# A new written-out order for one core, in which the fifth load waits for the first

## The chip, the cores and the metric

The kernel runs on one core of one Trainium2 chip. The metric is the time that the device takes for one launch, in microseconds. Three runs of the kernel before took 370.65, 370.40 and 370.61 us, the median is 370.61 us. The profile is of one further execution.

## What is computed

Three stages follow one another, on two sequences (batch 2) of 768 tokens.

1. Attention with 8 heads of 64 channels. Each query sees its neighbours at a distance under 16, and 24 summaries, one for each block of 32 tokens: the largest key and the mean value of the block. Softmax runs over both together.
2. A mixer on x (768 tokens x 512 channels): theta = x @ w_theta; y = w_tok_r @ (x cos theta) + w_tok_i @ (x sin theta); u = x + y; the stage gives u + relu(u @ w_ch).
3. A gated unit: h = gelu(x @ w_in), split into u and v of 512 channels; v is normalised over its channels, mixed over tokens by w_sg, scaled, biased, multiplied by u; the stage gives x + gated @ w_out.

## The kernel before

**A list of steps.** The program is cut into some 1,670 named steps, each on one engine. The function `op` registers a step. `play` walks a string, `PLAN`, and issues the steps in that order. A word of it reads `name.engine.place`: `k1.S.479` issues the load of the keys of pair 1 on SP (S) into place 479 of a byte-addressed area in SBUF; P is TensorE, V VectorE, A ScalarE, G GpSimd. For P, K, B and D kinds the place is a PSUM bank or a small buffer. So the order on each engine, which engine does a step that may run on several, and every buffer's place all come from `PLAN`. Nothing is scheduled at run time. A word with `~name` adds a wait on that earlier step; before the change this is used for GpSimd steps alone, to keep them behind a VectorE step.

**Pairs.** Heads go in pairs, eight pairs p = 0 to 7 (four of each sequence). A pair has one load of keys `kP` (128 x 768 f32), one of values turned `vTP` (the same size), two halves of queries `qP_0`, `qP_1` (128 x 384), and two of values by window `vP_0`, `vP_1` (96 x 774, as two transfers). All loads are issued by SP, in the order of `PLAN`.

**Steps of a pair's half.** `ksP` (VectorE) takes the block maxima of the keys. `SP_h` (TensorE, lines 636, 643, 650) makes the scores: 4 matmuls that write the masks, 24 with keys, 24 with block maxima. `mP_h` and `dP_h` (VectorE) find and subtract the maximum, `eP_h` (ScalarE) is the exponential, `PTP_h` (TensorE, line 674) transposes, `PtP_h` (ScalarE) copies out, `OP_h_0/1` (line 690) multiply by values, `nP_h` divides, `XP_h` (line 711) transposes. `vsP` (GpSimd for the first pairs, lines 583 and 585) sums values by block in five instructions, `vpP` (line 600) transposes the sums, `vmP` and `vrP_h` spread them into the value tiles, which the `O` steps read.

**Fillers.** `fill` is 97 matmuls without use before the first scores, `idleN` are matmuls of 480 columns without use (line 472), as many as the tuple `IDLE` says.

**The rest.** `th`, `y` (mixer), `ch`, `iv`, `iu`, `sg`, `o` are products in three fp32r matmuls each (lines 385 to 387). The weights of theta, `wthN`, come by load `wthNd` and three conversions. The number after each letter is the sequence. In the gated unit, `iv1_*` make v of the second sequence, `st1_*`, `sq1` and `rv1` its statistics, `vo1_i` the normalised tile i, `vn1_ih` and `vn1_il` its high and low part. `sg1_*_i` multiplies with tile i, `iu1_*` makes u, and `o0_*` is the last product of the first sequence.

Of the kernel before, what the change touches and what calls it, by code (L numbers as in the profile page):

```python
# [55 lines left out]
wth0t.A.2 vs2.G.2 e0_1.A vp2.P.3 vr0_0.G v0_1.S.1054 wth0r.V.1152 PT2_0.P.1 Pt2_0.A.1355 d1_1.V.3  # L56
k3.S.720 O0_0_0.P.6 q3_1.S.360 O0_0_1.P e2_1.A vT3.S.1536 n0_0.V.1.1632 vm2.A.1 idle2.P.0 PT0_1.P.0
O1_0_0.P.2 Pt0_1.A.96 O1_0_1.P X0_0.P.4 n1_0.V.0 xe0_0.V wth1d.S.832 v2_0.S.479 PT2_1.P.6 ks3.V.0
vr0_1.G~wth0r e1_1.A wth0h.A.1920 vs3.G.5~wth0r wth1t.A.0 v1_1.S.406 PT1_1.P.0 q3_0.S.2736 X1_0.P.4
O0_1_0.P.5 wth1r.V.687 Pt2_1.A.144 S3_1.P.2 S3_0.P.6 O0_1_1.P v3_0.S.1743 vr1_1.A Pt1_1.A.48  # L60
O1_1_0.P.0 O1_1_1.P wth0l.V m3_1.V.1 xh0_0.G.2208~wth0l vr2_0.G~wth0l d3_1.V.315 O2_0_0.P.2
O2_0_1.P wth1h.A.2696 xe1_0.A m3_0.V.4 d3_0.V.723 e3_1.A v2_1.S.783 vr2_1.G~wth0l wth2d.S.896
xh1_0.G.2064~wth0l vp3.P.1 n0_1.V.1.192 vm3.A.1 PT3_1.P.3 xl0_0.G~wth0l v3_1.S.1103 O2_1_0.P.1
O2_1_1.P n1_1.V.0 th0_0.P.6 e3_0.A Pt3_1.A.528 wth3d.S.2624 X0_1.P.7 n2_0.V.4 PT3_0.P.4
vr3_0.G~wth0l th2_0.P.0 vr3_1.G~wth0l wr1d.S.990 n2_1.V.0 X2_0.P.3 vT5.S.2448 wth2t.A.2 wr0d.S.1792
wth3t.A.1 Pt3_0.A.1055 O3_1_0.P.2 O3_1_1.P xl1_0.G xe2_0.A O3_0_0.P.5 O3_0_1.P k4.S.288 q4_1.S.1448
wi0d.S.1186 xe0_1.A X1_1.P.3 xh2_0.A.144 wth2r.V.736 wth1l.V wth2h.A.64 th2_1.P wth3r.V.2496
n3_0.V.1 X2_1.P.7 th0_1.P X3_0.P.4 q4_0.S.455 th1_0.P.5 vT4.S.2640 wri0d.S.1472 xl2_0.G~wth3r
th1_1.P wth2l.V wr0t.A.1 wri1d.S.2576 wth3h.A.0 wr1t.A.2 wth3l.V xe3_0.A th0_2.P th1_2.P
xh3_0.A.2064 xe2_1.A wr0r.V.1154 n3_1.V.2 th2_2.P X3_1.P.7 wi0t.A.1 ks4.V.1 xh0_1.G.2016~wr0r  # L70
xe1_1.A xl3_0.G~wr0r wr1r.V.544 xh2_1.A.864 th1_3.P th0_3.P wi0r.V.576 S4_0.P.1 v4_0.S.719 S4_1.P.3
th2_3.P xl0_1.V xl2_1.G~xl0_1 xe3_1.A xh1_1.G.144~xl0_1 th5_0.P.7 kk1.A.1888 rr1.V.1600 v4_1.S.1250
m4_0.V.5 xl1_1.G~xl0_1 d4_0.V.1299 th3_0.P.2 th4_0.P.5 wri0t.A.1 th3_1.P wr2d.S.2176
xh3_1.G.912~xl0_1 kk0.A.687 q7_0.S.1223 vs4.V.4 vp4.P.1 wri0r.V.1888 ab1_0.A.2144 wri1t.A.2
k6.S.1400 m4_1.V.1 d4_1.V.1747 xl3_1.G~wri0r wi0h.A.960 kk2.A.639 rr2.V.2496 th3_2.P ks6.V.1
q6_1.S.312 th3_3.P e4_0.A sc1_0.A PT4_0.P.3 vm4.A.1 wi0l.G~wri0r th4_1.P rr0.V.1792 th5_1.P
ab0_0.V.1824 th5_2.P q7_1.S.391 kk3.A.496 wri0h.G.1088~wri0r q6_0.S.2664 wri0l.G~wri0r wri1r.V.415
Pt4_0.A.2256 vs5.V.4 vr4_0.A S6_0.P.0 O4_0_0.P.6 v5_0.S.2399 rr3.V.1568 O4_0_1.P sc0_0.A vp5.P.4
e4_1.A th4_2.P zm1_0.G~wri1r v7_1.S.1487 vr4_1.G~wri1r PT4_1.P.2 th5_3.P wr0h.A.1984 ab2_0.A.447
vT6.S.671 k5.S.2544 zm0_0.G~wri1r zh0_0.G.832~wri1r Pt4_1.A.336 m6_0.V.0 wr0l.G~wri1r n4_0.V.4.2592  # L80
th4_3.P wi1d.S.2319 zl0_0.G~wri1r ks5.V.2 d6_0.V.626 q5_0.S.288 wri1h.G.768 X4_0.P.3 kk4.A.736
vm5.A.2 zh1_0.A.896 zl1_0.G rr4.V.2464 wi1t.A.2 wri2d.S.1728 O4_1_0.P.2 O4_1_1.P xe4_0.A S5_0.P.0
S6_1.P.4 vs6.V.4 y0_0_0_0.P.6.3 y0_0_0_1.P m5_0.V.0 wri1l.G d5_0.V.578 vp6.P.1 y0_0_1_0.P.0
n4_1.V.1.672 m6_1.V.0 d6_1.V.1843 k7.S.2256 y0_0_1_1.P kk5.A.512 q5_1.S.1351 S5_1.P.4 wr1h.A.1024
wr1l.G sc2_0.A y0_1_0_0.P e6_0.A wi1r.V.1186 e5_0.A ks7.V.0 vm6.V.1 PT5_0.P.1 vr5_0.A vT7.S.2128
wi1h.G.128~wi1r wi1l.G~wi1r wri2t.A.2 y0_1_0_1.P v6_0.S.1247 m5_1.V.4 Pt5_0.A.336 wr2t.A.0
d5_1.V.1403 rr5.V.288 vs7.V.4 S7_1.P.4 v5_1.S.1351 e5_1.A y0_1_1_0.P vr5_1.A e6_1.A PT5_1.P.1
wi2d.S.2311 zm2_0.G~wi1r zh2_0.G.832~wi1r y0_1_1_1.P zl2_0.G~wi1r m7_1.V.1 v7_0.S.1167 d7_1.V.1299
PT6_0.P.4 Pt5_1.A.464 O5_1_0.P.7 O5_1_1.P O5_0_0.P.1 Pt6_0.A.416 O5_0_1.P wri2r.V.1888 S7_0.P.4
wr2r.V.512 vr6_0.A wri2h.G.896~wr2r v6_1.S.591 n5_1.V.1 O6_0_0.P.2 n5_0.V.1 O6_0_1.P wri2l.G~wr2r  # L90
wr2h.A.2048 wr4d.S.2383 X5_1.P.1 e7_1.A m7_0.V.2 wr2l.G~wr2r vp7.P.7 wi2t.A.1 d7_0.V.419 xe5_1.A
vr6_1.G~wr2r vm7.A.2 y0_2_0_0.P e7_0.A n6_0.V.6 PT7_1.P.4 X5_0.P.7 wi5d.S.320 xe5_0.V wr5d.S.2240
Pt7_1.A.1296 PT7_0.P.1 vr7_1.G~wr2r Pt7_0.A.2128 vr7_0.G~wr2r PT6_1.P.4 wi2r.V.1218 X6_0.P.7
O7_0_0.P.2 wi2h.G.384~wi2r O7_1_0.P.1 O7_1_1.P Pt6_1.A.1439 ab2_1.V.2351 wi2l.G~wi2r ab1_1.A.2208
O7_0_1.P xe6_0.V wr4t.A.2 xh4_0.V.528 n7_1.V.1 O6_1_0.P.4 O6_1_1.P y0_2_0_1.P xh5_0.A.480 sc1_1.A
X7_1.P.7 n7_0.V.0 wr3d.S.1856 xl4_0.G~wi2r ab3_0.V.2544 n6_1.V.4 xl5_0.G~wi2r th8_0.P.5
ab3_1.V.1536 th8_1.P wr4r.V.1154 ab0_1.A.2112 X4_1.P.1 wr3t.A.1 xh6_0.V.1440 xe4_1.V ab4_0.A.608
th7_0.P.2 sc0_1.A xe7_1.V xl6_0.V wr3r.V.2144 sc2_1.A wi5t.A.0 wri3d.S.1280 y0_2_1_0.P X7_0.P.1
y0_2_1_1.P zm0_1.V th6_0.P.4 xe7_0.V X6_1.P.7 sc3_0.A xh4_1.G.1488~zm0_1 zm2_1.G~zm0_1 th7_1.P
xh7_0.A.528 xl7_0.V th7_2.P th6_1.P zh0_1.A.832 xe6_1.A zl0_1.V xh6_1.V.480 ab5_1.V.2176 wri3t.A.2  # L100
sc3_1.A xl4_1.G~zl0_1 xl6_1.V th8_2.P wri3r.V.640 th8_3.P xh5_1.A.1872 wr3h.A.1728 th7_3.P
kk7.A.1568 th6_2.P xl5_1.V wr3l.G~xl5_1 th6_3.P xh7_1.A.528 th11_0.P.1 zm1_1.V th11_1.P th9_0.P.7
th9_1.P th9_2.P wri4d.S.2112 wri5d.S.2383 kk6.A.1632 kk8.A.1600 zm3_0.V sc5_1.A th11_2.P rr7.V.1248
xl7_1.V th10_0.P.2 th10_1.P zm3_1.V wi5r.V.1312 rr6.V.1216 zh3_1.G.1920~wi5r ab6_0.V.320 rr8.V.1280
ab4_1.A.1568 th9_3.P th10_2.P wr4h.A.1472 wr4l.V zl3_1.V wri3h.A.448 th11_3.P zh3_0.G.64~zl3_1
wi3d.S.1600 wri4t.A.0 kk9.A.352 rr9.V.1664 zh1_1.G.2696~zl3_1 zl1_1.V zm5_1.V sc4_0.A ab8_1.A.1536
wr5t.A.1 wr5r.V.576 sc4_1.A wi5h.A.1344 ab6_1.V.1696 zl3_0.V th10_3.P wri4r.V.1152 zh2_1.A.1856
wi3t.A.1 wi3r.V.2112 wi3h.A.512 ab9_0.A.1184 zl2_1.G~wi3r wri3l.V wi3l.V wch0d.S.2240 sc6_0.A
wri5t.A.1 wi4d.S.2319 zm4_0.V y0_0_2_0.P.5.4 y0_0_2_1.P y0_0_3_0.P.7 y0_0_3_1.P y0_1_2_0.P
y0_1_2_1.P y0_1_3_0.P wri4h.A.1792 y0_1_3_1.P y0_2_2_0.P wch1d.S.2528 y0_2_2_1.P wri4l.V y0_2_3_0.P  # L110
y0_2_3_1.P wi5l.V zm4_1.G~wi5l wr5h.A.1408 zh4_0.A.2696 zh4_1.G.0~wi5l wri5r.V.1312 zm6_0.V
wi4t.A.2 y0_3_0_0.P wch2d.S.2112 wch2t.A.1 wr5l.V wi4r.V.2464 zl4_1.V ab5_0.A.1600 y0_3_0_1.P
ab8_0.V.2351 kk10.A.1152 y0_3_2_0.P y0_3_2_1.P y0_3_3_0.P zl4_0.G~zl4_1 zh5_1.G.832~zl4_1
wi4h.A.1856 rr10.V.2432 sc8_1.A kk11.A.639 y0_3_1_0.P ab9_1.A.2319 y0_3_3_1.P sc8_0.A wi4l.G~zl4_1
rr11.V.352 zh6_0.G.1920~zl4_1 y0_3_1_1.P zl5_1.V wri5h.A.64 wri5l.V wch0t.A.0 sc9_1.A sc6_1.A
sc5_0.A y0_4_2_0.P wch2r.V.2400 y0_4_2_1.P wch3d.S.576 zm8_0.G~wch2r y0_4_3_0.P ab7_0.V.1152
zm5_0.V wch1t.A.2 ab11_1.V.1280 wch0r.V.640 wch3t.A.1 zm8_1.V y0_4_0_0.P y0_4_3_1.P sc9_0.A
y0_5_2_0.P ab7_1.A.1632 zh5_0.A.2176 zm6_1.V y0_5_2_1.P y0_5_3_0.P wch1r.V.1312 y0_4_0_1.P
y0_4_1_0.P y0_4_1_1.P zh6_1.A.2240 y0_5_3_1.P zl5_0.V sc7_0.A zm7_0.G~zl5_0 zh7_0.A.0 ab11_0.A.1568
zm9_1.V ab10_1.A.2464 sc10_1.A zl7_0.V sc7_1.A y0_5_0_0.P y0_5_0_1.P winv2d.S.1216 zl6_0.V  # L120
# [1074 lines left out]
```

## Time and profile before

| | |
|---|---|
| median of the runs | 370.61 us |
| the profiled execution | 369.8 us |
| its span, first to last instruction | 368.1 us |
| TensorE matmul busy | 358.0 us (97%) |
| VectorE busy | 300.1 us (82%) |
| ScalarE busy | 215.2 us (58%) |
| GpSimd busy | 156.7 us (43%) |
| share of the chain that ended last | PE 89%, DMA 4%, DVE 2%, ACT 2% |

Some 1.7 us of the execution lie outside the span. A busy TensorE is one with a matmul in flight: matmuls overlap, so a step's cost is best read as the start of the next step less its own start. The chain is followed back from the last instruction; where it names an engine other than TensorE, TensorE was not what set the pace there.

### The profile page before, as it was taken

The page shows a single profiled execution, that of the slowest core. Times are in us where ns is not written, and L with a number is a line of the kernel's source. Part 1 is how long each engine was busy: PE and PEld are TensorE (multiplying, and loading weights), DVE is VectorE, ACT ScalarE, POOL GpSimd, SP SyncE. Part 2 cuts the span into 40 slices and gives each one's busy share as a digit, 9 for nine tenths or more (in the row PEclk, how much of TensorE's full clock was granted, in tenths as well). Part 3 has the DMA queues.
Part 4 walks back from the last instruction along what each step waited for, and adds up shares of the span by engine and source line. Part 5 has one row for each costly group of instructions (what it writes and reads, how often), then busy time and mean ns, then how long its engine had stood idle before and what let it go on. Part 6 is the DMA issues. An engine that isn't in the chain of part 4 may idle for free.

```text
span 368.1 us, 8188 instructions
## 1 busy us (share of the span) xinstructions
PE 358.0 (97%) x3237; PEld 330.9 (90%) x3237; DVE 300.1 (82%) x525; ACT 215.2 (58%) x414; POOL 156.7 (43%) x172
## 2 busy tenths in 40 slices
...
GB/s 249 334 300 379 343 231 284 153 207 116 59 164 179 57 2 239 46 116 1 2 0 2 43 59 45 42 88 58 144 0 2 0 3 57 58 2 0 61 69 215
DMA packets 16486, 40.53 MB, mean 110 GB/s; under 512 B 2240, under 2 KB 7872, under 8 KB 16448
## 3 DMA queue, kind: packets, MB, share of 16 engines
...
## 4 chain that ended last, share of the span: by engine, by line
PE 89%; DMA 4%; DVE 2%; ACT 2%; SPq 1%; POOL 1%; issue 0%; DVEq 0%
PE banks L385 27%; PE banks L386 26%; PE banks L387 26%; PE banks L690 3%; PE banks L674 2%; DMA page1F<-in_vT_dram 2%; PE banks L643 2%; DMA page14F<-in_qT_dram 2%; PE banks L711 1%; ACT banks L1026 1%; PE banks L650 1%; POOL page1F L583 1%; PE banks L636 1%; DVE page10F L1045 1%; SPq L568 1%
## 5 line engine op out<-in xcount | busy, mean ns | idle before, releaser
L372 ACT ACTIVATE page3F<-banks 128x384 f32<-128x384 f32 (+1 forms) x14 | 6.5, 468 | 19.6 <-PE banks L387 12.0
L656 DVE TENSOR_REDUCE small<-banks 128x6 f32<-128x720 f32 x16 | 14.4, 901 | 2.7 <-PE banks L650 2.6
L372 ACT ACTIVATE page1F<-banks 128x384 f32<-128x384 f32 (+1 forms) x13 | 7.7, 590 | 11.0 <-PE banks L387 9.6
L804 DVE TENSOR_TENSOR xT<-banks,xT 128x256 f32<-128x256 f32 (+1 forms) x16 | 8.1, 547 | 2.8 <-PE banks L387 2.8
L372 ACT ACTIVATE page7F<-banks 128x256 f32<-128x256 f32 (+2 forms) x15 | 7.0, 470 | 5.3 <-PE banks L387 5.2
L385 PE MATMUL banks<-page6R,page12R 128*128 128x384 f32 x24 | 8.0, 334 | 0.0
L386 PE MATMUL banks<-page6R,page12R 128*128 128x384 f32 x24 | 8.0, 334 | 0.0
L387 PE MATMUL banks<-page6R,page12R 128*128 128x384 f32 x24 | 8.0, 334 | 0.0
L380 POOL TENSOR_TENSOR page4R<-xT,page4R 128x384 fp32r<-128x384 f32 x3 | 3.1, 1021 | 11.4 <-DVE page6R L380 7.6
L1083 DVE SCALAR_TENSOR_TENSOR page1F<-banks,g_sb,page13F 128x384 f32<-128x384 f32 x10 | 6.0, 612 | 1.7 <-PE banks L387 1.6
L385 PE MATMUL banks<-page9R,page5R 128*128 128x384 f32 (+2 forms) x22 | 7.3, 333 | 0.0
L386 PE MATMUL banks<-page9R,page5R 128*128 128x384 f32 (+2 forms) x22 | 7.3, 331 | 0.0
L387 PE MATMUL banks<-page9R,page5R 128*128 128x384 f32 (+2 forms) x22 | 7.3, 330 | 0.0
L583 POOL TENSOR_TENSOR page8F<-page8F 128x384 f32<-128x384 f32 (+3 forms) x8 | 4.5, 564 | 6.0 <-DMA page8F<-in_vT_dram 5.6
L517 ACT ACTIVATE stage<-page11F 128x512 f16<-128x512 bf16 x6 | 4.7, 785 | 4.1 <-DMA page11F<-in_w_ch_dram 3.6
L380 POOL TENSOR_TENSOR page4R<-page1F,page4R 128x512 fp32r<-128x512 f32 (+1 forms) x3 | 4.4, 1480 | 5.7 <-ACT page4R L372 3.2
L875 POOL TENSOR_TENSOR page8F<-page1F,page8F 128x256 f32<-128x256 f32 x2 | 2.4, 1203 | 10.2 <-DVE page3F L875 6.2
L385 PE MATMUL banks<-page6R,page2R 128*128 128x384 f32 x20 | 6.7, 335 | 0.0
L386 PE MATMUL banks<-page6R,page2R 128*128 128x384 f32 x20 | 6.7, 335 | 0.0
L387 PE MATMUL banks<-page6R,page2R 128*128 128x384 f32 x20 | 6.7, 334 | 0.0
L875 POOL TENSOR_TENSOR page8F<-page12F,page3F 128x256 f32<-128x256 f32 x1 | 5.3, 5275 | 2.7 <-DVE page4R L380 2.7
L374 POOL TENSOR_SCALAR page7R<-xT 128x384 fp32r<-128x384 f32 (+1 forms) x2 | 1.4, 676 | 11.7 <-DVE page1F L1089 6.9
...
## 6 DMA issues: line engine op xcount, KB each, us to landing
page12F<-in_w_iT_dram SPq DMA_DIRECT2D x3, 511.8 KB, 4.3
page1F<-in_w_in_dram SPq DMA_DIRECT2D x3, 511.8 KB, 3.6
...
page1F<-in_w_sgT_dram SPq DMA_DIRECT2D x3, 384.0 KB, 3.2
page4F<-in_w_theta_dram SPq DMA_DIRECT2D x2, 511.8 KB, 6.1
page9F<-in_w_rT_dram SPq DMA_DIRECT2D x2, 511.8 KB, 5.9
page11F<-in_w_rT_dram SPq DMA_DIRECT2D x2, 511.8 KB, 5.9
page11F<-in_w_ch_dram SPq DMA_DIRECT2D x2, 511.8 KB, 4.8
```

Of the source, the lines that this page charges most:

```text
L372: ACT.activation(dst, src, AF.Copy)
L380: EN[e].tensor_tensor(out=lo, in0=src, in1=hi.bitcast(F32), op=ALU.subtract)
L385: PE.matmul(ps, ah, bh, start=first, stop=False, skip_group_check=True)
L386: PE.matmul(ps, ah, bl, start=False, stop=False, skip_group_check=True)
L387: PE.matmul(ps, al, bh, start=False, stop=last, skip_group_check=True)
L583: POOL.tensor_tensor(out=vv[:, :, :m], in0=vv[:, :, :m], in1=vv[:, :, m:2 * m], op=ALU.add)
L643: PE.matmul(s3(h)[sl(ab, 64), t, :WK], q[rr, sl(2 * t + ab, 64)], k[rr, FIRST[w]:FIRST[w] + WK], start=False, stop=True, skip_group_check= ...
L656: op(f"m{u}", "V", lambda e: DVE.tensor_reduce(out=m3(), in_=s4(), axis=AX.X, op=ALU.max, negate=True), after=[f"S{u}"], new=[(f"m{u}", "K ...
L674: PE.transpose(T(f"PT{u}")[:WC, h, sl(t)], T(f"P{u}")[:, 360 * h + t * WC:360 * h + (t + 1) * WC], ident)
L690: PE.matmul(ps[64 * ab:64 * ab + 64, o:o + 65], sb[:WC, x:x + 64], v[:WC, c:c + 65], start=True, stop=True)
L804: DVE.tensor_tensor(out=dst, in0=ps, in1=dst, op=ALU.add)
L875: op(f"{nm}+{j}", "VG", lambda e, j=j, p=p, q=q, o=o: EN[e].tensor_tensor(out=s(j)(), in0=p(), in1=q(), op=o), after=after + pre[j], cols= ...
```

## The change

The functions stay as they are. `IDLE` and the whole of `PLAN` change: the order of the steps on every engine, most places, and the engine of 185 steps out of some 1,670 (between VectorE, ScalarE and GpSimd). One filler step, `idle2`, goes; the first grows by two matmuls. The first sixteen loads before and after:

```
before: k1 q1_0 k2 vT1 q2_0 k0 q0_0 vT0 q2_1 q0_1 vT2 q1_1 v1_0 v0_0 wth0d v0_1 ...
after:  k1 q1_0 k0 k2 vT1~k1 q2_0 q0_0 vT0 q0_1 wth0d vT2 q2_1 v0_0 v1_0 q1_1 vT3 ...
```

`vT1.S.336~k1` is the fifth load. `play` gives it a wait on the landing of `k1`; SP works in order, so every later load is issued behind it. The beginning of the diff:

```diff
-IDLE = (6, 1, 1,)
+IDLE = (8, 1,)
...
-ones.V band.G k1.S.479 masks.G q1_0.S.240 warm.V.2716 identb.V fill.P.6 ks1.V.5 maskb.A S1_0.P.4
-m1_0.V.2 k2.S.1368 ks2.V.3 sets.G d1_0.V.195 vT1.S.1584 q2_0.S.599 k0.S.1296 ks0.V.4 idle0.P.0
-S2_0.P.6 m2_0.V.2 q0_0.S.1512 idle1.P.0 S0_0.P.0 d2_0.V.3 vT0.S.312 sums.G e1_0.A q2_1.S.288
-q0_1.S.72 vs1.G.1 vs0.G.0 vp1.P.4 vm1.A.0 vT2.S.1440 PT1_0.P.2 m0_0.V.1 S0_1.P.4 d0_0.V.2691
-Pt1_0.A.240 vp0.P.2 S2_1.P.6 q1_1.S.608 e2_0.A e0_0.A v1_0.S.2447 vr1_0.A PT0_0.P.0 m0_1.V.4
-d0_1.V.99 m2_1.V.1 d2_1.V.1798 S1_1.P.4 vm0.A.2 Pt0_0.A.192 v0_0.S.527 m1_1.V.4 wth0d.S.2112
...
+k1.S.2640 ones.V q1_0.S.1448 k0.S.1296 band.G warm.V.2716 k2.S.48 masks.G sums.G vT1.S.336~k1
+identb.V fill.P.6 q2_0.S.240 ks1.V.5 q0_0.S.599 ks0.V.4 maskb.A S1_0.P.4 ks2.V.3 vT0.S.144 sets.G
+idle0.P.0 S2_0.P.6 m1_0.V.2 d1_0.V.99 e1_0.A m2_0.V.0 d2_0.V.3 vs1.G.1 S0_0.P.0 vp1.P.2 m0_0.V.7
+vm1.A.0 q0_1.S.455 d0_0.V.2691 vs0.G.6 idle1.P.3 S0_1.P.2 e2_0.A PT2_0.P.6 m0_1.V.4 wth0d.S.656
+wth0t.A.2 e0_0.A vp0.P.5 vT2.S.1440 q2_1.S.1512 v0_0.S.591 vm0.A.2 S2_1.P.0 vr0_0.A PT0_0.P.4
+Pt0_0.A.2544 d0_1.V.195 v1_0.S.527 PT1_0.P.2 vs2.G.2 q1_1.S.360 S1_1.P.4 m2_1.V.8 Pt1_0.A.1536
...
```

TensorE's order at the start and around the statistics of the second sequence (the other engines' steps left out):

```
before: fill S1_0 idle0 S2_0 idle1 S0_0 vp1 PT1_0 S0_1 vp0 S2_1 PT0_0 S1_1 vp2 PT2_0 O0_0_0 ...
after:  fill S1_0 idle0 S2_0 S0_0 vp1 idle1 S0_1 PT2_0 vp0 S2_1 PT0_0 PT1_0 S1_1 O0_0_0 vp2 PT0_1 O0_0_1 O1_0_0 O1_0_1 PT2_1 X0_0 PT1_1 S3_1 O0_1_0 S3_0 ...

before: iv1_1C_1_1 iv1_1B_0_1 (14 steps of iu1) o0_0B_0_0 sg1_1_2_0 sg1_1_1_0 sg1_1_0_0 sg1_0_2_0 sg1_0_0_0 sg1_1_2_1 o0_1A_0_0 ...
after:  iv1_0C_1_0 iv1_0C_1_1 (14 steps of iu1, with o0_1A_0_0 and o0_0A_0_0 between them) o0_0B_0_0 sg1_1_2_0 sg1_0_2_0 sg1_0_0_0 sg1_1_2_1 sg1_0_0_1 ...
```

In that place `vn1_0h` and `vn1_0l` move from VectorE to GpSimd.

## Rows read from the trace of the kernel before

**Rows 1.** Busy us by stretch: PE, PEld, DVE, ACT, POOL, clock, DMA, GB/s
```profile
27.80:300.00 272.20, 272.20 (x2257) 249.91 (x2254) 223.02 (x398) 170.03 (x334) 118.39 (x112) 1.00 0.31 103
300.00:314.00 14.00, 13.08 (x75) 12.11 (x74) 12.29 (x24) 11.49 (x24) 7.97 (x7) 1.00 0.17 54
364.00:368.10 4.10, 0.00 (x0) 0.00 (x0) 0.51 (x1) 0.00 (x0) 0.00 (x0) 0.85 0.53 193
```

**Rows 2.** The chain that ended last, 0 to 30 us: start, us, what
```profile
4.05 7.67 DMA page1F<-in_vT_dram
21.21 5.54 DMA page14F<-in_qT_dram
```

**Rows 3.** TensorE's timeline, 1.5 to 28 us: start, us, line, operation, wait
```profile
1.55 3.42 PE L466 MATMUL banks<-page14F 128*128 128x40 bf16 x97 [1.55 <-DVE page14F L400]
4.89 0.35 PE L636 MATMUL banks<-maskb,identb 64*64 64x288 bf16 x4
5.99 1.39 PE L472 MATMUL banks<-maskb,identb 128*128 128x480 bf16 x6
7.31 0.32 PE L636 MATMUL banks<-maskb,identb 64*64 64x288 bf16 x4
8.73 0.72 PE L643 MATMUL banks<-page7F,page3F 64*64 64x96 f32 x24 [1.10 <-DMA page3F<-in_qT_dram]
9.70 0.38 PE L472 MATMUL banks<-maskb,identb 128*128 128x480 bf16 x1
10.01 0.32 PE L636 MATMUL banks<-maskb,identb 64*64 64x288 bf16 x4
11.93 0.28 PE L600 MATMUL banks<-ident,small 128*24 128x128 f32 x1
12.79 0.32 PE L636 MATMUL banks<-maskb,identb 64*64 64x288 bf16 x4
14.66 0.28 PE L600 MATMUL banks<-ident,small 128*24 128x128 f32 x1 [0.72 <-POOL small L585]
17.99 0.82 PE L674 MATMUL banks<-ident,page0F 128*120 128x128 f32 x6
25.46 0.32 PE L636 MATMUL banks<-maskb,identb 64*64 64x288 bf16 x4
27.76 0.57 PE L690 MATMUL banks<-page5F,page0F 120*64 120x65 f32 x12
```

**Rows 4.** Busy time by stretch, two early slices, columns as in rows 1
```profile
5.00:6.00 1.00, 1.00 (x53) 0.97 (x53) 0.00 (x0) 0.00 (x0) 0.00 (x0) 1.00 0.86 203
8.00:9.00 1.00, 0.27 (x12) 0.30 (x16) 0.89 (x2) 0.08 (x1) 0.82 (x1) 1.00 1.00 386
```

**Rows 5.** Loads: form, count, size of one, us from issue to landing
```profile
page2F<-in_kT_dram SPq DMA_DIRECT2D x1, 384.0 KB, 3.2
page11F<-in_w_theta_dram SPq DMA_DIRECT2D x1, 511.8 KB, 5.7
```

**Rows 6.** TensorE's timeline, 307 to 314 us, columns as in rows 3
```profile
307.88 0.33 PE L385 MATMUL banks<-page4R,page5R 128*128 128x384 f32 x1
308.93 0.45 PE L385 MATMUL banks<-page9R,page8R 128*128 128x384 f32 x1 [0.36 <-DVE page8R L377]
309.94 0.34 PE L385 MATMUL banks<-page9R,page8R 128*128 128x384 f32 x1
310.47 0.33 PE L385 MATMUL banks<-page9R,page8R 128*128 128x384 f32 x1
312.03 0.33 PE L385 MATMUL banks<-page0R,page2R 128*128 128x384 f32 x1
313.17 0.44 PE L385 MATMUL banks<-page11R,page0R 128*128 128x384 f32 x1 [0.46 <-DVE page3F L1065]
```

**Rows 7.** The same stretch on VectorE and on GpSimd: the low part of a tile
```profile
308.91 0.69 DVE L380 TENSOR_TENSOR page8R<-page3F,page8R 128x512 fp32r<-128x512 f32 x1
310.56 1.34 POOL L380 TENSOR_TENSOR page2R<-page3F,page2R 128x512 fp32r<-128x512 f32 x1
```

More of the change, by code (lines that the diff above doesn't have):

```diff
@@ L55 @@
-d0_1.V.99 m2_1.V.1 d2_1.V.1798 S1_1.P.4 vm0.A.2 Pt0_0.A.192 v0_0.S.527 m1_1.V.4 wth0d.S.2112
[L56 to L120, printed above, removed]
@@ L223 @@
-g0_0q2l.G o0_0B_0_0.P.5 wout1d.S.1375 vo1_1.A vn1_0h.V.1664 vn1_0l.V sg1_1_2_0.P.3 iu1_012.V.2600
-ut1_1_0g.A.264 sg1_1_1_0.P.4 vo1_4.A vo1_2.V vo1_3.V vn1_1h.G.384~vn1_0l vn1_2h.A.2432
-sg1_1_0_0.P.0 sg1_0_2_0.P.6 iu1_111.V.2688 iu1_011.V.664 vn1_3h.V.512 vn1_1l.G~vn1_0l sg1_0_0_0.P.1
-g0_1+2.G.2064~vn1_0l vn1_2l.V ut1_0_0g.A g0_1q1h.A.2112 vn1_3l.G~vn1_2l sg1_1_2_1.P o0_1A_0_0.P.2
-vn1_4h.V.2304 wout3d.S.704 vo1_5.A sg1_1_0_1.P sg1_0_0_1.P sg1_0_2_1.P sg1_1_2_2.P sg1_1_2_3.P
-o0_0A_0_0.P.7 wout1t.A.1 sg1_0_2_2.P sg1_1_0_2.P vn1_4l.V sg1_0_0_2.P sg1_0_0_3.P sg1_0_0_4.P
```

330 lines of the change are left out of this document (200 added, 130 removed).

## The prediction

> **What bounds the kernel now.** I read the chain that ended last first, then TensorE's busy time by stretch, then its timeline where the two disagree. From 27.8 to 300 us TensorE is busy all 272.2 us [rows 1]: in that time the order of the other engines costs nothing, and the new order has nothing to win there, only to lose. Time that isn't products lies in three places. At the start the chain runs through two loads, `vT0` (issued at 4.05, landed 7.67 later, at 11.72) and `q3_0` (21.21 + 5.54 = 26.75) [rows 2]. Around 308 us the statistics of the second sequence hold TensorE up [rows 1, 6]. The end, after the last product at 363.9, is one VectorE step and a store [rows 1], and both orders close with a product, a VectorE step and a store, so I put 0 on the end.
>
> What TensorE loses at the start comes from its timeline [rows 3]. A scores step takes 5.99 - 4.89 = 1.10 where its data are there. The first filler takes 7.31 - 5.99 = 1.32. `S2_0` takes 9.70 - 7.31 = 2.39, so it loses 1.29 (to `q2_0`). The single filler takes 0.31, and there is a second one alike. `S0_0` takes 11.93 - 10.01 = 1.92, loses 0.82. `S0_1` to `vp0` is 14.66 - 12.79 = 1.87, loses 0.77 (the block sums of `vT0`). `S3_0` takes 27.76 - 25.46 = 2.30, loses 1.20 (`q3_0`). Together 1.32 + 1.29 + 0.62 + 0.82 + 0.77 + 1.20 = 6.0 us. This is all that the new start can win.
>
> **The change, part by part.** *Landings after the change.* The first eight loads are the same set, so if the transfers keep their pace the eighth, `vT0`, lands at 11.72 in both [rows 2]. Inside the set `k0` moves ahead. A load of keys has 128 x 3072 B = 0.393 MB [rows 5], a half of queries 0.197, a half of window values 96 x 3096 B = 0.297, a theta weight 0.524 [rows 5]. Behind `q2_0` there then come `q0_0` and `vT0`, 0.59 MB; at the 386 GB/s of 8 to 9 us [rows 4] that is 1.5 us, so `q2_0` lands at 10.2 (before: in time for the 8.73 start [rows 3]). `vT1` lands 0.79 MB before 11.72, at 9.7. For what follows I take the pace of before: from `vT0` to `q3_0` the loads were five halves of queries, three of keys or values, five halves of window values and two theta weights, 4.70 MB in 26.75 - 11.72 = 15.0 us, 0.3125 MB/us. After the change: `q2_1` comes after `q0_1`, `wth0d`, `vT2`: 1.31 MB, 15.9. `q1_1` 0.79 MB more, 18.4. `k3` 1.51 more, 23.3. `q3_0` 0.79 more, 25.8. `v3_0` 2.24 more, 33.0.
>
> *TensorE after the change.* To 5.99 as before: `k1` and `q1_0` stay first and second. The filler of 8 costs 8/6 x 1.32 = 1.76, to 7.75. `S2_0` waits for `q2_0`: its key matmuls start 0.1 after 10.2, and from there to the next step it is 0.97 (8.73 to 9.70 [rows 3]), so 11.3: it takes 3.5, loses 2.4. `S0_0` to 12.4 without a wait (`q0_0` at 10.7). `vp1` needs the sums of `vT1`: 9.7 + 2.9 (before: 11.72 to 14.66 [rows 2, 3]) = 12.6, loses 0.2. The single filler 0.3. `S0_1` to 14.1, `PT2_0` 0.8 [rows 3], to 15.0; `vp0` waits for GpSimd, which takes `vT0` only after `vT1`: 12.6 + 2.8, loses 0.45. `S2_1` waits for `q2_1` at 15.9, loses 0.25. `S1_1`, near 18.6, finds `q1_1` there. `S3_0`, near 25.5, waits for `q3_0`: loses 0.2. `O3_0_0`, near 34, has `v3_0` at 33.0 and two ScalarE copies behind it: 0.5 by estimate. Together 1.76 + 2.4 + 0.2 + 0.3 + 0.45 + 0.25 + 0.2 + 0.5 = 6.1. The start is a wash: +0.1. One late load (`q3_0`) is relieved, and the price is paid earlier, at `S2_0`, behind which TensorE's whole queue stands.
>
> *The added wait.* The fifth load is issued at about 4.0 (0.78 + 3.2 [rows 5]), not at 2.2, and all later ones behind it. At that time `k0` and `k2`, 0.79 MB, are still to come, 2 us at 386 GB/s, so the transfers don't run dry: cost 0. What it may win is the slow slice: 203 GB/s at 5 to 6 us, against 386 later [rows 4]. If the slice is slow because seven or eight loads were issued by then, the wait gives back up to 2 x (1 - 203/386) = 0.95 us (two such slices, by estimate from the one row). Bounds 0 and -0.95. I take 0, because later slices with as many loads under way run at full pace.
>
> A rule speaks against a gain: by the Trainium skill's page "DMA: Bandwidth & Descriptors", section "Queues, rings and completion order", each DMA engine consumes one queue's descriptors in ring order, and all these loads are on SP's queue; then later loads can't take pace from the first, and the term is 0. In this trace the first keys land 3.2 after issue, before all else [rows 5], which agrees.
>
> *The statistics of the second sequence.* Before, `o0_0B_0_0` to `sg1_1_2_0` takes 308.93 - 307.88 = 1.05, the next 1.01, `sg1_1_2_1` to `o0_1A_0_0` 1.14, where a free step takes 310.47 - 309.94 = 0.53 [rows 6]: 1.6 us lost. After, two more output products stand ahead of the first `sg1` step, 2 x 0.53 = 1.06 more cover: the first two losses (1.0) go. But `vn1_0`'s low part moves to GpSimd, 1.34 for 0.69 [rows 7], so about 0.4 of it is late again, and the bank waits of the third kind (0.6 [rows 6]) stay, since `sg1_0_2_0` and `sg1_0_0_0` take banks that VectorE empties after two normalisations. Gain 1.6 - 1.0 = 0.6; bounds: all 1.6 won, or 0.8 lost if both bank waits are full ones.
>
> *Everything else.* 185 steps change engine and most places change. Between 34 and 300 us all that lies beside a TensorE that never waits [rows 1]; cost 0, from -0.2 to +1 if one late weight shows.
>
> *Sum.* +0.1 - 0.6 + 0 = -0.5. Against the profiled execution's 369.8 this is 369.3. That execution is 0.8 below the median of the runs, 370.6, so the runs should give **370.1 us**.
>
> **Rivals.** (1) *The early slow slice goes away* with the wait. For it: pace doubles two slices later [rows 4], when SP has issued all it may. Against it: the ring order. Every landing comes 0.95 earlier and TensorE with it: 370.1 - 0.95 = 369.1.
>
> (2) *The clock falls in the longer wait.* TensorE now stands still from about 8.0 to 10.3, longer than any wait before (1.10 [rows 3]). For it: clock is lost after work ends; of 364 to 368.1 the granted share is 0.85 [rows 1], which is 1.2 us at the lower level (1.2 GHz), so it fell some 2.9 us after the last product; and at the start 40 columns took 3.42/97 us = 35 ns [rows 3], that same level, until about 5.0. Against: 2.3 is under 2.9. If it falls, it is as at the start: 3.4 us of work at half pace [rows 3] before it rises, 1.7 lost, more (to 3.5) as the steps up to 16 us have gaps. 370.1 + 2.2 = 372.3. It decides as soon as a granted clock under 1 shows between 8 and 16 us.
>
> The Trainium skill's page "TensorE: Matmul & The Clock Gate", section "What's actually happening", says that idling brings the clock to half; no stretch here shows it inside the kernel.
>
> (3) *The landings are later than by bytes, or the statistics lose more*: +1 on one of the two, 371.1. For it: SP may also stand at a place that isn't free (`v0_0` goes where `q0_0` was, so it waits for `S0_0`).
>
> (4) *The wait does nothing*, since `k1` would have landed first anyhow, and the new order is worth only its fillers, one matmul more: 370.8.
>
> **How the numbers follow.** Forecast 0.42, rivals 0.25, 0.13, 0.12, 0.08. A run can tell 0.2%, 0.74 us: faster is under 369.87, slower over 371.35. The forecast gives 0.14 faster, 0.24 same, 0.04 slower; rival 1 gives 0.22 and 0.03; rival 2 0.13 slower; rival 3 0.05 same and 0.07 slower; rival 4 0.06 and 0.02. Faster 0.36, but the bounds of the start and the statistics reach further down (-0.95, -1.6) than up, so I move 0.08 there from same: 0.44, 0.30, 0.26. Range 367.8 (both lower bounds nearly whole) to 372.2 (the clock).
>
> **What would show it.** `S2_0`'s key matmuls should start at 10.3 (rival 1: 9.4 or before), with `k0` landed by 7. If TensorE waits there under 1 us, the landings by bytes are wrong. `S3_0` should wait under 0.5. The stretch 300 to 314 should hold some 13.6 us of products instead of 13.08. A granted clock under 1 before 300 us is rival 2. A wait of TensorE between 40 and 300 us would make the zero for everything else wrong.

## The result and the profile after

The change makes the kernel slower by 0.56%: 372.71 us (median) against 371.10 us for the kernel before, run beside it; the ratio is 1.0056, 95% interval 1.0034 to 1.0078. It is an estimate of its own from the runs; the ratio of the two medians, 1.0043, lies within its interval. The forecast was 370.1, with the range up to 372.2. The profiled execution of after has a span of 371.8 us (before: 368.1), at a granted clock of 0.999. Its distance, 3.7 us, is more than that of the runs (2.1 us by the ratio): the one profile of before lies below its median, that of after above.

TensorE's losses, taken as in the prediction (start of the next step less own start, less what the same pair of steps takes where nothing waits), fillers counted as lost:

| us | before | after | forecast of the difference | measured |
|---|---|---|---|---|
| to 30 us | 6.42 | 9.12 | +0.1 | +2.70 |
| 30 to 250 us | 0.38 | 2.83 | 0 (-0.2 to +1) | +2.45 |
| 250 to 300 us | 0.14 | 0.23 | 0 | +0.09 |
| from 300 us | 1.63 | 0.28 | -0.6 (-1.6 to +0.8) | -1.35 |

The sum, +3.89, is where TensorE's last product ends: 367.79 for 363.91 us. Two new losses outweigh the one gain.

*The start.* SP's timeline of after (start, us, line, operation, tiles):

```profile
8.09 0.43 SPq L561 DMA_DIRECT2D page7F<-in_qT_dram  x1
12.17 1.93 SPq L567 DMA_DIRECT2D page3F<-in_vW_dram  x2
14.15 1.15 SPq L567 DMA_DIRECT2D page2F<-in_vW_dram  x2
15.40 0.53 SPq L561 DMA_DIRECT2D page1F<-in_qT_dram  x1
```

From 8.52 to 12.17 SP issues nothing: next in its order is `v0_0.S.591`, into 591 to 639, where `q0_0` (599 to 622) lies until `S0_0` has read it; `S0_0`'s last matmul ends at 12.13. What that does to the transfers shows in busy time by stretch, the answer to [rows 4] (columns as in [rows 1]; last column GB/s):

```profile
5.00:6.00 1.00, 1.00 (x28) 0.99 (x32) 0.00 (x0) 0.00 (x0) 0.00 (x0) 1.00 1.07 338
8.00:9.00 1.00, 0.48 (x6) 0.11 (x4) 1.00 (x2) 0.00 (x0) 0.00 (x0) 1.00 0.92 312
13.00:14.00 1.00, 0.88 (x49) 0.88 (x50) 0.96 (x3) 0.93 (x3) 0.92 (x2) 1.00 0.53 168
14.00:15.00 1.00, 1.00 (x25) 0.77 (x17) 1.00 (x2) 0.73 (x2) 0.77 (x4) 1.00 0.19 42
```

The early slow slice is gone (203 GB/s before), and at 14 to 15 us, where before had 267, the DMA engines are nearly idle (share 0.19). `q1_1`, issued at 15.40, lands at 20.07 (forecast 18.4), `k3` at 26.19 (forecast 23.3). TensorE's timeline, the answer to [rows 3]:

```profile
6.44 1.79 PE L471 MATMUL banks<-maskb,identb 128*128 128x480 bf16 x8
10.15 0.72 PE L642 MATMUL banks<-page0F,page1F 64*64 64x96 f32 x24 [1.68 <-DMA page1F<-in_qT_dram]
20.12 0.73 PE L642 MATMUL banks<-page13F,page1F 64*64 64x96 f32 x24 [1.52 <-DMA page1F<-in_qT_dram]
26.33 0.73 PE L642 MATMUL banks<-page11F,page0F 64*64 64x96 f32 x24 [0.58 <-DMA page11F<-in_kT_dram]
27.23 0.55 PE L649 MATMUL banks<-small,page0F 64*64 64x24 f32 x24 [0.17 <-DVE small L572]
28.16 0.57 PE L689 MATMUL banks<-page5F,page1F 120*64 120x65 f32 x12 [0.39 <-issue]
```

The first row, the filler, starts at 6.44 where before had 5.99. That is scatter, worth 0.45 of the +2.70: in all the profiles of either order it starts anywhere from 5.79 to 6.82. The second row is `S2_0`'s wait for `q2_0`, forecast and there. The third is `S1_1` (loses 1.75 in all), the next three `S3_1` up to the step behind it (1.67): neither was forecast. The chain that ended last runs through the same loads, where [rows 2] had `vT0` and `q3_0`:

```profile
4.03 5.53 DMA page1F<-in_vT_dram
17.39 8.80 DMA page11F<-in_kT_dram
```

*Near 55 us.* VectorE (first fence) stands 3.14 us in front of `vs5`, the block sums of `vT5`. The releaser that it names had long been done; `vT5` landed at 54.27. `d4_1`, behind `vs5` on VectorE, empties the bank that `O4_0_0` writes, so TensorE (second fence) stands after `vp5`:

```profile
54.36 0.95 DVE L579 TENSOR_REDUCE small<-page8F 128x24 f32<-128x768 f32 x1 [3.14 <-PE banks L385]
```

```profile
55.37 0.28 PE L599 MATMUL banks<-ident,small 128*24 128x128 f32 x1
57.17 0.92 PE L689 MATMUL banks<-page7F,page2F 120*64 120x65 f32 x24 [1.52 <-DVE page3F L661]
```

SP had stood again, from 41.41 to 46.19: `q7_1.S.288` goes where `q4_0` lies until `S4_0` ends at 46.12, and `vT5` is the third load behind it.

*The statistics of the second sequence*, and the end; busy time by stretch answering [rows 1], then TensorE's timeline answering [rows 6]:

```profile
30.00:300.00 270.00, 268.10 (x2213) 244.85 (x2212) 224.68 (x391) 168.46 (x325) 107.20 (x103) 1.00 0.32 105
306.00:320.00 14.00, 13.99 (x81) 13.58 (x80) 11.80 (x25) 11.80 (x22) 10.46 (x8) 1.00 0.12 37
367.80:371.80 4.00, 0.00 (x0) 0.00 (x0) 0.56 (x1) 0.00 (x0) 0.00 (x0) 0.92 0.43 154
```

```profile
314.71 0.33 PE L384 MATMUL banks<-page9R,page12R 128*128 128x384 f32 x1
314.89 0.34 PE L385 MATMUL banks<-page9R,page12R 128*128 128x384 f32 x1
315.24 0.45 PE L386 MATMUL banks<-page9R,page12R 128*128 128x384 f32 x1
```

All that is left of 1.63 us is 0.28 in `sg1_1_2_0`, whose third matmul waits for the low part. The end is as it was.

### The profile page after: what moved, and what is told of

The parts are those of the page before. It is cut to its first block, busy times and chain, and to the rows that moved or that the text cites. A ratio compares the mean times of both kernels' runs of the same rounds, so it can differ in the third digit from the quotient of the medians.

```text
span 371.8 us, 8181 instructions
## 1 busy us (share of the span) xinstructions
PE 359.1 (97%) x3238; PEld 331.6 (89%) x3238; DVE 302.5 (81%) x526; ACT 216.2 (58%) x416; POOL 151.6 (41%) x169
## 4 chain that ended last, share of the span: by engine, by line
PE 87%; DMA 5%; DVE 2%; ACT 2%; SPq 1%; issue 1%; POOL 1%; DVEq 0%
PE banks L384 26%; PE banks L385 26%; PE banks L386 26%; PE banks L689 3%; DMA page11F<-in_kT_dram 2%; PE banks L673 2%; DMA page1F<-in_vT_dram 1%; PE banks L710 1%; PE banks L642 1%; PE banks L649 1%; DMA page13F<-in_kT_dram 1%; ACT banks L1025 1%; SPq L567 1%; POOL page1F L582 1%; PE banks L635 1%
## 5 line engine op out<-in xcount | busy, mean ns | idle before, releaser
L371 ACT ACTIVATE page3F<-banks 128x384 f32<-128x384 f32 (+2 forms) x16 | 7.6, 476 | 20.1 <-PE banks L386 17.9
L371 ACT ACTIVATE page1F<-banks 128x384 f32<-128x384 f32 (+2 forms) x13 | 7.2, 556 | 17.0 <-PE banks L386 16.5
L379 POOL TENSOR_TENSOR page14R<-page3F,page14R 128x512 fp32r<-128x512 f32 x2 | 2.6, 1289 | 15.2 <-issue 14.0
L384 PE MATMUL banks<-page9R,page12R 128*128 128x384 f32 x24 | 8.2, 340 | 0.1
L386 PE MATMUL banks<-page9R,page12R 128*128 128x384 f32 x24 | 8.1, 339 | 0.0
L385 PE MATMUL banks<-page9R,page12R 128*128 128x384 f32 x24 | 8.0, 334 | 0.0
L668 ACT ACTIVATE page0F<-page0F 128x720 f32<-128x720 f32 x3 | 2.4, 805 | 9.4 <-DVE page0F L661 9.3
L1082 DVE SCALAR_TENSOR_TENSOR page13F<-banks,g_sb,page13F 128x384 f32<-128x384 f32 x8 | 4.9, 614 | 3.0 <-PE banks L386 3.0
L384 PE MATMUL banks<-page0R,page10R 128*128 128x512 f32 (+1 forms) x19 | 6.9, 364 | 0.0
L386 PE MATMUL banks<-page0R,page10R 128*128 128x512 f32 (+1 forms) x19 | 6.6, 346 | 0.0
L385 PE MATMUL banks<-page0R,page10R 128*128 128x512 f32 (+1 forms) x19 | 6.6, 345 | 0.0
L1109 POOL TENSOR_TENSOR page1F<-page1F,xT 128x384 f32<-128x384 f32 x3 | 3.1, 1023 | 7.9 <-DVE page1F L1109 7.4
L384 PE MATMUL banks<-page12R,page2R 128*128 128x384 f32 x18 | 6.1, 336 | 0.0
L385 PE MATMUL banks<-page12R,page2R 128*128 128x384 f32 x18 | 6.0, 335 | 0.0
L386 PE MATMUL banks<-page12R,page2R 128*128 128x384 f32 x18 | 6.0, 335 | 0.0
L379 POOL TENSOR_TENSOR page10R<-page3F,page10R 128x512 fp32r<-128x512 f32 x3 | 3.9, 1292 | 4.8 <-ACT page10R L371 4.8
```

Source lines behind the costliest of these rows:

```text
L371: ACT.activation(dst, src, AF.Copy)
L379: EN[e].tensor_tensor(out=lo, in0=src, in1=hi.bitcast(F32), op=ALU.subtract)
L384: PE.matmul(ps, ah, bh, start=first, stop=False, skip_group_check=True)
L385: PE.matmul(ps, ah, bl, start=False, stop=False, skip_group_check=True)
L386: PE.matmul(ps, al, bh, start=False, stop=last, skip_group_check=True)
L1082: DVE.scalar_tensor_tensor(out=T(gf)[:, s], in0=T(bk)[:, :384], scalar=g_sb[:, f:f + 1], in1=T("bsg")[:, s], op0=ALU.mult, op1=ALU.add)
```

## The experiments

Theory A: SP, working in order, stands at places that are still read; loads behind it are issued late, the transfers run dry and later steps wait. Its rivals: B, the loads are late by the bytes ahead of them in the new order; C and D, the added wait costs, or wins, by itself. Ratios are to the kernel before, with 95% intervals. Landings and waits are from each kernel's own profile.

**Two places (e1_two_places).**

```diff
-v0_0.S.591 ... q1_1.S.360
+v0_0.S.2447 ... q1_1.S.264
```

> The kernel after, with two loads given places that nothing used before: v0_0 (2447 for 591) and q1_1 (264 for 360). Order and engines stay. Theory A (standing queue): SP stands from 8.5 to 12.2 us because v0_0's place still holds q0_0, which S0_0 reads, and the 16 DMA engines run out of loads (42 GB/s at 14 to 15 us). Then v0_0 is issued near 9.6, q1_1 near 12.2 (15.4 before the edit), q1_1 lands near 17.3 (20.07) and k3 near 22.2 (26.19), the slice under 200 GB/s between 13 and 15 us goes, S1_1 and S3_1 no longer wait (1.75 and 1.67 us), and the time is 3 us under the kernel after, 369.5 to 370 where that takes 372.7. Theory B (bytes ahead): the loads are late only because 1.1 MB more stand ahead of q1_1 in the new order; then q1_1 lands later than 19 and the time moves by less than 0.7 us.

371.28 us, ratio 1.0012 (0.9991 to 1.0034), so by the ratios 1.6 us under after, where 3 were expected. SP's timeline, and busy time by stretch:

```profile
9.08 1.05 SPq L567 DMA_DIRECT2D page12F<-in_vW_dram  x2
11.62 0.58 SPq L561 DMA_DIRECT2D page1F<-in_qT_dram  x1
```

```profile
13.00:14.00 1.00, 1.00 (x50) 0.97 (x40) 0.97 (x2) 1.00 (x2) 0.92 (x2) 1.00 1.10 312
14.00:15.00 1.00, 0.81 (x10) 0.45 (x9) 1.00 (x2) 0.72 (x2) 0.84 (x4) 1.00 1.11 252
```

The dry slice is gone, `q1_1` lands at 18.18, `k3` at 22.88, and `S1_1` and `S3_1` wait no more. Same bytes, same order: B is out. The losses to 30 us fall by 2.36, not 3.4, since TensorE loses 1.56 at `S2_1` in this profile, on something new (last section).

**The added wait alone (e2_no_wait, e3_before_with_wait).**

```diff
 e2, on the kernel after:
-vT1.S.336~k1
+vT1.S.336
 e3, on the kernel before:
-q2_0.S.599
+q2_0.S.599~k1
```

> The kernel after without the added wait: the fifth load is issued at once. Theory A: what the early loads win by it (338 to 356 GB/s at 4 to 7 us) is lost again at 7 to 9 us, so that vT0 lands within 0.4 us of 11.5 and the time stays within 0.7 us of the kernel after. Theory C (the wait is what costs): the eight loads land as in the kernel before or sooner, S2_0 waits less, and the time is 1 us or more under the kernel after. Theory D (the wait wins): the slice of 203 GB/s is back at 5 to 6 us and every landing to 12 us is 0.9 later, the time 0.7 us or more over the kernel after.

> The kernel before with nothing changed but one wait: its fifth load (q2_0) waits for the landing of its first (k1). Theory A: the slice of 203 GB/s at 5 to 6 us goes, k2 lands near 6.2 (7.10) and vT1 near 7.2 (8.10), but q2_0, issued near 4.0, lands near 9 (8.60), and vT0 within 0.4 us of 11.72; the time stays within 0.7 us of the kernel before. Theory C: 1 us or more over the kernel before. Theory D: all landings to 12 us 0.9 sooner, TensorE's losses at the start 0.5 to 0.9 us smaller, and the time as much under the kernel before.

Without the wait 372.34 us, ratio 1.0056 (1.0031 to 1.0081), that of after; `vT0` lands at 11.63 for 11.51. With the wait in the kernel before 370.92, ratio 1.0005 (0.9989 to 1.0021); `vT0` lands at 11.38 for 11.72. C is out, and of D no more than 0.4 us is left by e3's interval. Busy time by stretch of the kernel before with the wait:

```profile
5.00:6.00 1.00, 1.00 (x53) 0.87 (x46) 0.06 (x1) 0.00 (x0) 0.00 (x0) 1.00 0.99 368
6.00:7.00 1.00, 1.00 (x6) 0.39 (x4) 1.00 (x2) 0.00 (x0) 0.14 (x1) 1.00 0.69 217
```

Here the slow slice comes one us later. And after without its wait has all eight loads issued by 5.01 and still 295 GB/s at 5 to 6 us: the slice is no matter of how many loads are issued alone. `k1` lands at 3.72 to 4.04 in all fourteen profiles, whatever is issued behind it.

The ring order that the prediction cites from the Trainium skill's page "DMA: Bandwidth & Descriptors", section "Queues, rings and completion order", agrees with that.

**Later places (e4_place_q7_1, e5_all_places).**

```diff
 e4, on the kernel after:
-q7_1.S.288
+q7_1.S.1250
 e5, on e1, also:
-q3_1.S.72 q3_0.S.2664 wri1d.S.1792 q7_1.S.288 vT5.S.1584 wi1d.S.1472
+q3_1.S.288 q3_0.S.576 wri1d.S.1728 q7_1.S.1250 vT5.S.2176 wi1d.S.2528
```

> The kernel after, with one later load moved: q7_1 (1250 for 288, where q4_0 still lies until S4_0 has run). Theory A: SP stands from 41.4 to 46.2 us at that place, vT5 behind it lands at 54.27, VectorE stands 3.14 us in front of its block sums, and O4_0_0 on TensorE waits 1.5 us for the bank that VectorE then empties late. With the free place q7_1 is issued before 43, vT5 lands before 52, the two losses at 54 to 57 us (0.3 and 1.7) go, and the time is 1.5 to 2 us under the kernel after. Theory B: vT5 is late by the bytes ahead of it; it lands after 53.5, the wait at 55.7 us stays above 1 us, and the time moves by less than 0.7 us.

> The kernel after with eight loads of the first 60 us at places that come free long before: v0_0, q1_1, q3_1, q3_0, wri1d, q7_1, vT5, wi1d. Order and engines stay. Theory A (SP stands at places in use, and the transfers run dry behind it): no pause of over 1 us in SP's issues between 8 and 16 us, none from 41 to 49 us that a place explains; S1_1 and S3_1 wait under 0.3 us, the wait of 1.5 us behind vp5 near 55 us goes, and the wait for wi1d near 62 us (1.6 us with q7_1's place alone) shrinks under 0.8. The time is 3 us under the kernel after, so 0.2 to 0.5% under or level with the kernel before. Theory B (bytes ahead): with the places free the loads still land as late, the later waits come back in full, and the time stays within 0.7 us of the kernel after with two places moved (0.12% over the kernel before).

e4: 372.78 us, ratio 1.0041 (1.0013 to 1.0068): not told from after, so the 1.5 to 2 us expected didn't come. `vT5` lands at 50.17 and the loss behind `vp5` goes, as A has it; but then ScalarE (first fence) stands for `wi1d`, whose own place is in use, and TensorE (second) behind it for `xe4_0`:

```profile
63.12 0.77 ACT L516 ACTIVATE stage<-page7F 128x512 f16<-128x512 bf16 x1 [3.99 <-DMA page7F<-in_w_iT_dram]
```

```profile
64.37 0.47 PE L384 MATMUL banks<-page5R,page4R 128*128 128x512 f32 x1 [1.57 <-ACT xT L371]
```

e5: 370.52 us, ratio 0.9997 (0.9977 to 1.0018): 2.2 us under after, level with before. `wi1d` lands at 58.37, the losses from 30 to 250 us are 0.87 (2.83). So eight places take back the whole slowdown. The 3 us expected were too many; at the start of this profile 1.21 us went to a stand like e1's.

**The products at the statistics (e6_products_back, e9_before_products).**

```diff
 e6, on the kernel after (TensorE):
-o0_1A_0_0 iu1_0C_1_0 o0_0A_0_0 iu1_0C_1_1 o0_0B_0_0 sg1_1_2_0 sg1_0_2_0 sg1_0_0_0 sg1_1_2_1
+iu1_0C_1_0 iu1_0C_1_1 o0_0B_0_0 sg1_1_2_0 sg1_0_2_0 sg1_0_0_0 sg1_1_2_1 o0_1A_0_0 o0_0A_0_0
 e9, on the kernel before (TensorE; VectorE's iu1_111, iu1_011 ahead of vo1_2):
-o0_0B_0_0 sg1_1_2_0 sg1_1_1_0 sg1_1_0_0 sg1_0_2_0 sg1_0_0_0 sg1_1_2_1 o0_1A_0_0 ... o0_0A_0_0
+o0_0B_0_0 o0_1A_0_0 o0_0A_0_0 sg1_1_2_0 sg1_0_2_0 sg1_0_0_0 sg1_1_1_0 sg1_1_0_0 sg1_1_2_1
```

> The kernel after with one part of the stage at 314 us undone: the two output products o0_1A_0_0 and o0_0A_0_0 stand behind sg1_1_2_1 again, as before the change, and no longer ahead of the first sg1 step. If it is these two products (2 x 0.52 us) that cover the statistics of the second sequence, TensorE's loss at the first sg1 step rises from 0.28 to 1.2 to 1.4 us, and last-product time minus start of the stage rises by about 1.0. If it is the moves between engines (vn1_0 to GpSimd, other elementwise steps) that did it, the loss stays under 0.6.

> The kernel before with one part of the change alone, that at the statistics of the second sequence: the output products o0_1A_0_0 and o0_0A_0_0 go ahead of the first sg1 step, iu1_111 and iu1_011 on VectorE go ahead of vo1_2, and the four steps concerned exchange banks (2 with 4, 0 with 7, from there to the end). The start and all else stay. If the two products are what covers the statistics, TensorE's losses near 308 to 312 us (0.52, 0.49 and 0.62 us) fall from 1.63 to under 0.6, and the time is 1.0 to 1.4 us (0.3 to 0.4%) under the kernel before. If the gain there belongs to the engine moves of the change, the losses stay over 1.2 and the time within 0.4 us.

e6, from its profile alone: 0.28 becomes 1.26 us, in this row of TensorE's timeline (its L320 is L386 of after):

```profile
312.74 0.44 PE L320 MATMUL banks<-page9R,page12R 128*128 128x384 f32 x1 [0.91 <-POOL page12R L313]
```

So the two products are the cover. e9: 370.25 us, ratio 0.9989 (0.9966 to 1.0012), not told from before, where 0.3 to 0.4% was expected. In its profile the losses at the statistics fall from 1.63 to 0.88, not under 0.6: `sg1_1_2_3` is late next, by 0.72, for a low part that GpSimd makes (TensorE's timeline; L320 is L387 of before). That profile also holds a stretch at the lower clock (27.94 to 31.35), which is no part of these losses:

```profile
318.19 0.44 PE L320 MATMUL banks<-page9R,page2R 128*128 128x384 f32 x1 [0.45 <-POOL page2R L313]
```

**When a stand costs (e7_before_two_places, e11_before_standing).** The kernel before stands too, from 7.44 to 9.82, at `q1_1`'s place.

```diff
 e7, on the kernel before:
-q1_1.S.608 ... v2_0.S.479
+q1_1.S.144 ... v2_0.S.1250
 e11, on the kernel before:
-q1_1.S.608
+q1_1.S.1512
```

> The kernel before with two loads at places that are free early: q1_1 (144 for 608, where q2_0 lies until S2_0 has run) and v2_0 (1250 for 479). Theory A: SP no longer stands from 7.4 to 9.8 us and from 17.2 to 19.1, the slices of 267 to 301 GB/s between 12 and 15 us rise over 340, q3_0 lands near 25.5 (26.75) and S3_0 waits under 0.4 us (1.2), so the time is 0.8 to 1.2 us under the kernel before. Theory B: landings and time as in the kernel before, within 0.4 us.

> The converse test: the kernel before with one place changed so that SP stands longer. q1_1 goes to 1512, where q0_0 lies until S0_0 has run at 11.9 us, instead of 608, free after S2_0 at 9.7. Order, bytes and engines are those of the kernel before. Theory A (a long stand runs the transfers dry): SP stands from 7.4 to about 11.9, only two loads are under way at the end of it, a slice under 200 GB/s shows between 13 and 16 us, all later loads land 1.5 to 2 us later, S3_0 waits some 3 us (1.24), and the time is 1.2 to 2 us over the kernel before. Theory B (bytes and order alone set the landings): the time stays within 0.4 us of the kernel before.

e7: 371.11 us, ratio 0.9990 (0.9960 to 1.0019). `q1_1` is issued at 8.43 instead of 9.82 and lands at 15.29 instead of 14.80; `S3_0` loses 1.51. A is wrong for this stand: no cost shows. e11: 373.33 us, ratio 1.0079 (1.0055 to 1.0103), 2.9 us over before with one place changed. Its SP timeline, busy time by stretch, and TensorE's timeline:

```profile
6.26 0.33 SPq L559 DMA_DIRECT2D page7F<-in_vT_dram  x1
12.17 0.33 SPq L562 DMA_DIRECT2D page7F<-in_qT_dram  x1
```

```profile
12.00:13.00 1.00, 1.00 (x20) 0.80 (x18) 0.97 (x2) 0.27 (x1) 0.95 (x1) 1.00 0.17 61
14.00:15.00 1.00, 0.24 (x5) 0.09 (x1) 0.99 (x2) 0.57 (x2) 0.84 (x4) 1.00 0.30 107
```

```profile
21.71 0.54 PE L674 MATMUL banks<-ident,page0F 128*120 128x128 f32 x3 [1.39 <-ACT page0F L669]
```

The wait isn't where I put it (`S3_0` loses 0.71): the late `wth0d`, landed at 20.21 for 18.20, holds ScalarE, and `PT0_1` waits for the exponential. Behind that wait the granted clock is 0.50, TensorE's lower level (1.2 GHz):

```profile
22.61:26.02 3.41, 3.41 (x34) 2.95 (x33) 1.90 (x7) 2.61 (x5) 0.05 (x1) 0.50 1.00 323
```

From `O1_0_0` to `PT1_1`, about this stretch, TensorE falls from 2.22 to 3.55 us behind the kernel before. So some 1.3 of the 2.9 us, an estimate from this one profile, are the clock's, which leaves 1.6 for the late landings, within the 1.2 to 2 expected. None of the six runs has a mean granted clock over 0.995.

The three stands differ in what was still under way at their end: before 4.4 us of landings (9.82 to 14.23), after 2.6 (12.17 to 14.74), e11 1.6 (12.17 to 13.81). The first load after the stand took 2.90 us to land in after and 2.96 in e11. So the stand was free where the loads already issued outlasted it by more than that, and cost time in the two cases where they did not; three cases agree with this, no more is shown.

**Another start (e8_places_and_order).** The loads alone, against e5; the rest of the edit is in the words below.

```diff
-k1 q1_0 k0 k2 vT1~k1 q2_0 q0_0 vT0 q0_1 wth0d vT2 q2_1 v0_0 v1_0 q1_1 vT3 wth1d q3_1 k3
+k1 q1_0 k2 q2_0 k0~k1 q0_0 vT1 vT0 q0_1 q2_1 q1_1 vT2 v0_0 v1_0 wth0d q3_1 k3 vT3 wth1d
```

> The kernel with eight places moved, and a new order of the start: loads k1 q1_0 k2 q2_0 k0 q0_0 vT1 vT0 q0_1 q2_1 q1_1 vT2 v0_0 v1_0 wth0d q3_1 k3 vT3 wth1d (the fifth still waits for the first), TensorE S1_0, a filler of 6, S2_0 S0_0 PT1_0 S0_1 vp1 PT2_0 S2_1 vp0 PT0_0 S1_1, no second filler; ks0 behind d1_0 on VectorE, wth0t behind Pt0_0 on ScalarE. If the start is bound by when each load is wanted, S2_0 starts by 7.7 with a wait under 0.5 us, S1_1 ends by 18.5 (20.5 with the two places alone, 21.1 in the kernel after), k3 lands by 19.5, and the time is 1 to 2 us under the kernel before. If the start is bound by the bytes that have to land in any order, the wait only moves, to vp1 and vp0 and then to the O steps, and the time stays within 0.7 us of the eight places alone.

370.96 us, ratio 1.0008 (0.9981 to 1.0036), level with e5. `S2_0` waits no more and `k3` lands at 19.28, but `S1_1` ends at 20.2: `S0_0` now loses 1.03, `S0_1` 0.82, `S2_1` 1.22, `PT0_0` 1.55, the last since `S1_1` takes the bank that ScalarE empties behind `PT0_0`; 0.85 of `S2_1`'s is a stand like e1's. The wait moved.

**The better version (e10_products_and_q3_0, e13_best).**

```diff
 e10, on e9:
-v2_0.S.479 ... v1_1.S.406 ... q3_0.S.2736
+q3_0.S.2736 v2_0.S.479 ... v1_1.S.406
 e13, on e10 (TensorE):
-sg1_1_2_2 sg1_1_2_3 sg1_0_2_2 sg1_1_0_2 sg1_0_0_2
+sg1_1_2_2 sg1_0_2_2 sg1_1_0_2 sg1_0_0_2 sg1_1_2_3
```

> The kernel before with the products ahead of the sg1 step and, besides, the load q3_0 issued ahead of v2_0 and v1_1. If S3_0 waits for q3_0 only because 0.6 MB of later loads stand ahead of it, q3_0 lands near 25 (26.75), S3_0 loses under 0.3 us (1.24), up to 0.5 us of it comes back at O1_1_0, whose values v1_1 land later, and the time is 0.5 to 0.9 us under the kernel with the products alone. If the whole of it comes back at the O steps, the two are level.

> The kernel before with the two products ahead, q3_0 ahead of v2_0 and v1_1, and one product more moved: sg1_1_2_3 goes behind sg1_0_0_2, three products later, since it waited 0.72 us for the low part of tile 3 from GpSimd. If that wait has nothing behind it that comes late as well, TensorE's losses after 300 us fall from 0.88 to under 0.3 and the time is 0.4 to 0.7 us under the kernel with the products and q3_0 alone, 0.4 to 0.5% under the kernel before. If another low part is late next (tile 4 or 5), the loss moves there and the time stays level.

e10: 369.64 us, ratio 0.9970 (0.9956 to 0.9985); `q3_0` lands at 25.70 and `S3_0` loses nothing, though `S3_1` ahead of it loses 0.87. e13: 369.13 us, ratio 0.9948 (0.9928 to 0.9968): faster than both kernels. Its losses after 300 us are 0.53, not under 0.3, of which 0.37 at a later step.

## Why the prediction was wrong

*The step that failed* is "For what follows I take the pace of before", with "so the transfers don't run dry: cost 0" ahead of it. I looked for a dry stretch behind the added wait and found none, rightly; I didn't walk the same queue on to `v0_0`. Rival 3 named that very place, at +1 us and 0.12. Landing times by bytes held as long as SP ran: `q2_0` forecast at 10.2, landed 10.02; `vT0` 11.72 and 11.51; `q2_1`, the first by the pace of before, came early (15.9 and 14.74). Behind the stand they are late by 1.7 (`q1_1`) and 2.9 us (`k3`). With the two places free (e1) the same loads land at 18.18 and 22.88, within 0.5 us of the forecast 18.4 and 23.3: what failed is the stand left out, not the count of bytes.

*Everything else*, at "cost 0, from -0.2 to +1", failed by the same mechanism at 41 us. "A TensorE that never waits" [rows 1] is what the old order gave; 185 moved steps and new places void it, and the loads' places could be walked in the new order. The rise of 2.45 us is more than its bound of +1.

*The wait itself:* cost 0, right (e2, e3), though without it the fifth load is issued at 2.65 (e2), not at 2.2. *The early slow slice:* I gave rival 1 a chance of 0.25; it went away as that rival says, but `vT0` landed only 0.21 us earlier, less than the scatter (e1, with the same first loads, has 11.04), and e3's slice only moved. What sets it stays open.

*`S2_0`:* forecast to take 3.5 us, took 2.83 (10.99 - 8.16). *The statistics:* right in mechanism and sign, mis-sized: -1.35 for -0.6. The moved low part left 0.28 late, not 0.4, and of the 0.6 of bank waits that I kept nothing stayed.

*The clock* (rival 2): in after's profile the granted clock is 1.00 in every early stretch above. TensorE stood 1.68 us before 10.15, not the 2.3 forecast, so the rival has no part in these losses. Other profiles do show what it describes. In e2 TensorE stood 2.40 us in `S2_0`, until 10.29, and then (busy time by stretch; the clock is third from the end):

```profile
11.28:14.69 3.41, 3.41 (x81) 2.76 (x77) 3.34 (x5) 2.10 (x4) 2.94 (x8) 0.50 0.63 238
```

The same level shows again in e2 (28.34 to 31.75, behind a wait of 1.26 us that ended at 25.96), in e9 (27.94 to 31.35, behind one of 1.13 that ended at 26.55) and in e11 (1.39, until 21.71), while after's waits of 1.68 and 1.52 us brought none. So "2.3 is under 2.9" was no argument against the rival. That idling can bring the clock to half agrees with what the prediction cites for it from the Trainium skill's page "TensorE: Matmul & The Clock Gate", section "What's actually happening".

Is the slowdown then the clock's? Of after's 22 runs 12 had a mean granted clock of 0.997 or more, with a median of 372.20 us; of the 101 runs of before beside the experiments 64 had, with a median of 370.41. At that clock the kernels are 1.8 us apart, no less than the medians of all runs (1.6), so the clock is not the cause.
